# Gated linear attention with a gated projection on one core: attention in 64x64 blocks with a state at mid-chunk, one layout of v, y moved with its halo, and a new order of the work

## The chip, the cores and the metric

The kernel runs on one core of one Trainium2 chip. The metric is device time in microseconds (us), the median of several runs. Engines are named as in the profile: PE is TensorE (PEld its weight loads), DVE is VectorE, ACT is ScalarE, POOL is GpSimd, SP is SyncE, which only issues transfers here. In this kernel every engine's instructions are chained in the order in which the program is written, so each engine runs a fixed list.

## The reference

```python
f = 1 / (1 + exp(-f_logit))                       # B=4, H=8, S=768, D=48
for t in range(S):
    state = f[:, :, t, :, None] * state + einsum('bhd,bhe->bhde', k[:, :, t], v[:, :, t])
    y[:, :, t] = einsum('bhd,bhde->bhe', q[:, :, t], state)
x = y.transpose(0, 2, 1, 3).reshape(B, S, H * D)  # 4 x 768 x 384
gate = sigmoid(sum_k conv_w[k] * x shifted by 4 - k)   # 5 taps, per channel
out = (gate * (x @ w_val)) @ w_out                # two 384 x 384 products
```

## The kernel before

The 768 positions are six chunks of 128 (`NC`, `C`); a chunk is handled in two halves `h` of two batches each, and the eight heads of a batch lie as four pairs, one head on partitions 0 to 47 and one on 64 to 111. So a half holds eight pairs (`HP`).

Per chunk c the gates go through `pexp`, `pln`, a running sum (`csum` on PE in chunks 0 and 1, `scan` on DVE later) and `exp1`, `exp2`, the running product and its inverse; `pmulq` and `pmulk` scale q and k by them. With q and k scaled, a chunk's attention is plain products. `ktrans` transposes k on PE, `kevac` copies it out. `scores` makes k'q for 64-row blocks: the block on the diagonal, masked by `mask` (DVE), and the block of the first half of the chunk's keys against its second half of queries, copied by `cross` (ACT). `dstate` makes the whole chunk's addition to the state, which `stend` (DVE) adds and `stmul` (POOL) multiplies by the decay. `apply` sums four kinds of matmul into y: n = 0 and 1 from the state at the chunk's start, n = 2 and 3 from the masked blocks and v. Its output is written in 32-partition strips, in the place that x has in the projection, so that `xevac` (ACT) copies it straight to x (`XF`) and `halo` (POOL) copies the four positions before the chunk. For these strips v is loaded in two layouts, `vb` (in_v, with zero columns) and `vs` (in_vn).

The projection (numbered 0 to 4, and 5 and 6 for the two halves of the last chunk) takes x: `msplit` and `mlow` cut it in a high and a low part, `conv` (PE) or `mlast` and `mconv` (ACT, DVE) make the five taps, `gate` the sigmoid, `mval` the product with w_val, `mmul` the gating, `mhigh` and `mrest` the split of that, `mout` the product with w_out, `mstore` and `out` the result. The weights come as float64 and are rounded on the chip (`wload`, `weight`, eight steps each on POOL, ACT and DVE).

A float32 matmul is two records on PE with a weight load each; one in the split format (`mval`, `mout`) or a transpose is one. The whole order is one list, `PROGRAM`, of pieces such as `scores 1 2`: what is written first stands first on each engine that it uses. Loads are issued on SP with two rules (`begin`): each waits for the load four before it, and from the 16th on also for the PE instruction written just before it. `busy n` writes n matmuls on a constant, which nothing reads.

```python
for at, other in ((EARLY, PE.last), (FLIGHT, loads[n - FLIGHT] if n >= FLIGHT else None)):
```

All instructions carry the line of the helper that records them (L123 before, L140 after the change); tiles' names tell them apart: `banks<-qb,kb` is `scores`, `banks<-asb,vb` and `banks<-qb,st` are `apply`, `banks<-vs,ksb` is `dstate`, `banks<-ident,kb` is `ktrans`, `banks<-below,e` is `csum`, `banks<-xf,WD` is `conv`, `banks<-xH,wvT` is `mval`, `banks<-rg,woT` is `mout`, `banks<-keep` is `busy`.

Of the kernel before, what the change touches and what calls it, by code (L numbers as in the profile page):

```python
# [54 lines left out]
2; wload 4; loadw 0 1; loadq 1 0; wload 5; loadq 1 1; weight 0; pexp 0 2; pexp 0 1; pln 0 2; pln 0 1; csum 0 1; csum 0
2; exp2 0 0; pexp 1 0; exp1 0 0; exp2 0 1; pmulk 0 0; pmulq 0 0; pmulk 0 1; ktrans 0 0; exp1 0 1; pln 1 0; csum 1 0;
weight 1; exp2 0 2; exp1 0 2; pmulq 0 1; scores 0 1; kevac 0 0; pmulk 0 2; csum 1 1; dstate 0 0; exp2 1 0; weight 1;
exp1 1 0; okc 0; pmulq 0 2; scores 0 2; mask 0 1; weight 1; weight 1; weight 1; cross 0 1; weight 0; weight 0; weight
0; weight 0; weight 1; weight 0; scores 0 0; exp2 1 1; exp1 1 1; scores 0 3; mask 0 2; cross 0 2; ktrans 0 1; mask 0
0; cross 0 0; apply 0 0 3; pmulk 1 0; mask 0 3; pmulk 1 1; kevac 0 1; dstate 0 1; weight 2; weight 0; loadw 1 0; loadw  # L60
1 1; ktrans 1 0; weight 1; cross 0 3; weight 2; weight 1; weight 3; apply 0 0 2; ktrans 1 1; okc 1; weight 2; stend 0
1; stend 0 0; kevac 1 0; loadf 2 0; wload 6; apply 0 1 3; apply 0 1 2; pmulq 1 0; pmulq 1 1; xevac 0 0; weight 3;
weight 2; weight 2; weight 2; weight 3; weight 3; kevac 1 1; apply 1 0 0; scores 1 1; xevac 0 1; msplit 0; scores 1 0;
mask 1 1; weight 3; mask 1 0; dstate 1 1; dstate 1 0; weight 2; cross 1 1; scores 1 2; cross 1 0; apply 1 0 1; stend 1
1; stend 1 0; mlow 0; weight 3; pexp 2 0; pln 2 0; wload 7; loadv 1 1; loadk 2 0; loadk 2 1; loadw 2 0; apply 1 0 2;
apply 1 0 3; loadq 2 0; weight 2; weight 4; conv 0; weight 4; weight 3; xevac 1 0; scan 2 0; weight 4; mask 1 2; apply
1 1 0; cross 1 2; stmul 1 1; weight 3; weight 5; stmul 1 0; halo 1; exp2 2 0; exp1 2 0; loadf 3 0; loadq 2 1; loadv 3
0; loadw 2 1; wload 8; loadq 3 0; scores 1 3; loadv 2 0; loadk 3 1; loadv 2 1; loadk 3 0; gate 0 1; mval 0 1; mval 0
0; scan 2 1; weight 4; weight 4; pmulk 2 0; weight 5; gate 0 0; ktrans 2 0; exp2 2 1; weight 4; weight 5; weight 5;
mask 1 3; cross 1 3; mmul 0 0; exp1 2 1; weight 4; apply 1 1 1; apply 1 1 2; apply 1 1 3; mval 0 2; pmulk 2 1; weight  # L70
5; weight 5; pmulq 2 1; pmulq 2 0; ktrans 2 1; kevac 2 0; pexp 3 0; scores 2 0; xevac 1 1; mmul 0 2; apply 2 0 0; mmul
0 1; dstate 2 0; pln 3 0; kevac 2 1; scores 2 2; mask 2 0; cross 2 0; halo 2; weight 4; weight 6; scores 2 1; scan 3
0; mask 2 2; mask 2 1; dstate 2 1; msplit 1; cross 2 2; apply 2 1 0; weight 6; cross 2 1; scores 2 3; stend 2 0;
weight 6; weight 6; mask 2 3; weight 5; mhigh 0 0; exp2 3 0; cross 2 3; apply 2 1 1; apply 2 0 1; apply 2 0 2; apply 2
1 2; conv 1; apply 2 1 3; apply 2 0 3; weight 6; stend 2 1; weight 6; mrest 0 0; mlow 1; mhigh 0 1; exp1 3 0; mrest 0
1; mval 1 1; pmulk 3 0; mhigh 0 2; mrest 0 2; gate 1 0; stmul 2 0; weight 5; wturn 0; stmul 2 1; pmulq 3 0; apply 3 0
0; xevac 2 1; scores 3 0; xevac 2 0; scores 3 1; scan 3 1; okc 2; mlast 2 0; mmul 1 1; mconv 2 0 0; mlast 2 1; weight
6; weight 6; mconv 2 1 0; mconv 2 0 1; loadv 3 1; loadf 4 0; loadq 3 1; loadv 4 0; loadw 3 0; loadk 4 0; loadv 4 1;
loadw 3 1; mval 1 0; gate 1 1; mval 1 2; exp2 3 1; mask 3 0; cross 3 0; exp1 3 1; mmul 1 0; pmulk 3 1; mconv 2 1 1;
mask 3 1; mlast 2 2; cross 3 1; msplit 2; mout 0 0; ktrans 3 0; ktrans 3 1; mstore 0 0; mout 0 2; mmul 1 2; mconv 2 0  # L80
2; okc 3; mconv 2 1 2; pmulq 3 1; mconv 2 1 3; mconv 2 2 0; mconv 2 2 1; mconv 2 2 2; mconv 2 2 3; mout 0 1; pexp 4 0;
pln 4 0; kevac 3 0; mstore 0 2; mhigh 1 1; kevac 3 1; apply 3 0 1; apply 3 0 2; apply 3 0 3; mrest 1 1; scan 4 0;
apply 3 1 0; scores 3 3; xevac 3 0; scores 3 2; out 0 0; wturn 1; out 0 2; loadq 4 0; dstate 3 1; mask 3 2; mask 3 3;
mstore 0 1; mhigh 1 2; cross 3 2; dstate 3 0; cross 3 3; wturn 2; loadk 4 1; loadq 4 1; apply 3 1 1; apply 3 1 2;
apply 3 1 3; loadw 4 0; out 0 1; exp2 4 0; mhigh 1 0; exp1 4 0; stend 3 1; mrest 1 2; mrest 1 0; mconv 2 0 3; stend 3
0; pmulk 4 0; pmulq 4 0; stmul 3 1; stmul 3 0; halo 3; mout 1 0; mout 1 2; loadf 5 0; apply 4 0 0; gate 2; xevac 3 1;
halo 4; mlast 3 0; mlast 3 1; scores 4 0; scores 4 1; mstore 1 0; mlast 3 2; mstore 1 2; mlow 2; mval 2 0; loadq 5 0;
loadk 5 0; out 1 0; loadk 5 1; loadv 5 1; out 1 2; loadq 5 1; loadv 5 0; loadw 4 1; mval 2 2; mconv 3 1 0; mconv 3 0
0; scan 4 1; mconv 3 1 1; mmul 2 0; mconv 3 0 1; exp2 4 1; exp1 4 1; okc 4; mask 4 1; mout 1 1; cross 4 1; mmul 2 2;
mconv 3 2 0; pmulq 4 1; mask 4 0; pexp 5 0; pmulk 4 1; mhigh 2 0; ktrans 4 0; mval 2 1; mhigh 2 2; cross 4 0; pln 5 0;  # L90
kevac 4 0; apply 4 0 1; apply 4 0 2; apply 4 0 3; apply 4 1 0; ktrans 4 1; mmul 2 1; mhigh 2 1; mrest 2 0; mrest 2 2;
mrest 2 1; mout 2 1; scan 5 0; scan 5 1; mconv 3 0 2; mconv 3 2 1; mstore 1 1; mout 2 2; kevac 4 1; xevac 4 0; mstore
2 1; msplit 3; mlow 3; mout 2 0; scores 4 2; scores 4 3; mask 4 2; mask 4 3; mconv 3 0 3; out 1 1; out 2 1; exp2 5 1;
mstore 2 2; out 2 2; dstate 4 1; exp2 5 0; exp1 5 0; mstore 2 0; out 2 0; dstate 4 0; cross 4 2; cross 4 3; exp1 5 1;
apply 4 1 1; apply 4 1 2; apply 4 1 3; stend 4 1; stmul 4 1; pmulq 5 1; mconv 3 1 2; apply 5 1 0; mval 3 0; mconv 3 1
3; mconv 3 2 2; stend 4 0; mval 3 1; mconv 3 2 3; pmulk 5 1; pmulq 5 0; scores 5 2; xevac 4 1; gate 3; mlast 4 1; mmul
3 1; scores 5 3; pmulk 5 0; mval 3 2; halo 5; stmul 4 0; mlast 4 0; mask 5 3; cross 5 3; scores 5 0; mmul 3 0; mask 5
2; cross 5 2; mhigh 3 0; apply 5 1 1; apply 5 1 2; apply 5 0 0; apply 5 1 3; mmul 3 2; mrest 3 0; mhigh 3 2; mhigh 3
1; mlast 4 2; mrest 3 2; mrest 3 1; mout 3 1; mconv 4 0 0; mask 5 0; xevac 5 1; scores 5 1; cross 5 0; conv 6; mask 5
# [739 lines left out]
```

## Time and profile before

| what | us |
|---|---|
| median of 3 runs (lowest, highest) | 211.53 (209.95, 212.02) |
| the profiled execution, its span | 211.4 |
| its last matmul for the output ends | 204.1 |
| PE busy (records) | 182.7 (3732 and as many weight loads) |
| DVE busy | 145.5 |
| ACT busy | 130.2 |
| POOL busy | 36.6 |
| chain that ended last: PE, transfers, issue | 69%, 21%, 5% of the span |

The profiled execution is one run of the program and stands within 0.1 us of the median, so its rows add up to the time that is predicted. "Issue" in the chain is time in which an engine waited for nothing that the profile shows. The last 7.2 us of the span, from the last output's copy on, hold the landing of the last transfers and the test of a flag that sends rare inputs to a slow path.

### The profile page before, as it was taken

To read this page: it belongs to the slowest core of one execution; us is meant where nothing else is said; L and a number is where in the kernel's file an instruction comes from. 1 tells how busy PE (TensorE), PEld (TensorE's weight loads), DVE (VectorE), ACT (ScalarE), POOL (GpSimd) and SP (SyncE) were. 2 spreads that over 40 slices of the span, in tenths; PEclk is the share of its full clock that TensorE was granted. 3 is DMA by queue.
4 is the path that set the end of the run, shared out by engine and by line. 5 is a ranking of instruction groups with operands and counts; after the bars stand their busy time and mean duration, and the time that the engine had idled before them with its cause. 6 is when DMAs were issued, how large, how long until landed. Compare 5 with 4: busy or idle time off the path is not lost.

```text
span 211.4 us, 8218 instructions
## 1 busy us (share of the span) xinstructions
PE 182.7 (86%) x3732; PEld 149.6 (71%) x3732; DVE 145.5 (69%) x196; ACT 130.2 (62%) x188; POOL 36.6 (17%) x45
## 2 busy tenths in 40 slices
...
GB/s 197 334 264 342 346 368 210 284 8 289 319 363 381 288 15 3 6 99 409 338 286 122 288 240 173 386 352 108 6 2 3 6 3 101 0 3 3 132 215 11
DMA packets 12713, 38.61 MB, mean 183 GB/s; under 512 B 1537, under 2 KB 2945, under 8 KB 12161
## 3 DMA queue, kind: packets, MB, share of 16 engines
...
q8 instruction: 30, 0.49, 0.9%
...
## 4 chain that ended last, share of the span: by engine, by line
PE 69%; DMA 21%; issue 5%; SPq 1%; ACT 0%
PE banks L123 69%; DMA vb<-in_v 7%; DMA vs<-in_vn 6%; DMA qb<-in_q 3%; DMA raww<-in_wv 3%; DMA kb<-in_k 2%; SPq L123 1%; ACT qb L123 0%
## 5 line engine op out<-in xcount | busy, mean ns | idle before, releaser
L123 ACT ACTIVATE e<-e 112x1024 f32<-112x1024 f32 (+4 forms) x32 | 39.8, 1247 | 4.0 <-DMA e<-in_ft 3.4
L123 PE MATMUL banks<-xH,wvT 128*128 128x512 f32 x90 | 30.8, 404 | 0.0
L123 DVE SCALAR_TENSOR_TENSOR pre<-xf,cws,pre 128x512 f32<-128x512 f32 x36 | 27.3, 782 | 0.4
L123 PE MATMUL banks<-asb,vb 64*32 64x64 f32 (+3 forms) x1152 | 24.8, 261 | 2.1 <-issue 2.1
L123 PEld LDWEIGHTS banks<-asb,vb 64*32 64x32 f32 (+1 forms) x1152 | 22.4, 115 | 5.1 <-issue 4.1
L123 PE MATMUL banks<-rg,woT 128*128 128x512 f32 (+1 forms) x108 | 24.8, 371 | 0.0
L123 DVE TENSOR_TENSOR kb<-kb,e 112x1024 f32<-112x1024 f32 (+1 forms) x13 | 16.0, 1235 | 10.3 <-DMA kb<-in_k 10.3
L123 PE MATMUL banks<-vs,ksb 128*48 128x64 f32 x320 | 12.8, 242 | 11.6 <-DMA vs<-in_vn 5.9
L123 DVE TENSOR_TENSOR asb<-banks,tri 128x512 f32<-128x512 f32 x24 | 16.1, 683 | 7.7 <-PE banks L123 7.7
L123 PE MATMUL banks<-qb,kb 48*64 48x128 f32 (+1 forms) x768 | 19.8, 248 | 1.8 <-issue 1.8
L123 PEld LDWEIGHTS banks<-qb,kb 48*64 48x64 f32 x768 | 17.6, 133 | 5.1 <-issue 3.8
L123 POOL TENSOR_TENSOR st<-st,e 112x512 f32<-112x512 f32 x8 | 11.0, 1380 | 57.9 <-DVE st L123 34.6
L123 PEld LDWEIGHTS banks<-vs,ksb 128*48 128x48 f32 x320 | 11.4, 140 | 12.8 <-issue 10.1
L123 PEld LDWEIGHTS banks<-rg,woT 128*128 128x128 f32 x108 | 17.8, 188 | 3.4
L123 PEld LDWEIGHTS banks<-xH,wvT 128*128 128x128 f32 x90 | 16.9, 188 | 4.4 <-issue 0.2
L123 DVE TENSOR_TENSOR qb<-qb,e 112x1024 f32<-112x1024 f32 (+1 forms) x13 | 16.4, 1272 | 3.9 <-DMA qb<-in_q 2.3
L123 ACT COPY asb<-banks 128x256 f32<-128x256 f32 x24 | 8.8, 372 | 16.5 <-DVE asb L123 15.2
L123 DVE TENSOR_TENSOR_SCAN e<-keep,e 112x1024 f32<-112x1024 bf16 x8 | 18.3, 2304 | 0.0
L123 PE MATMUL banks<-xL,wvT 128*128 128x512 f32 x45 | 17.7, 394 | 0.0
L123 ACT COPY xf<-banks 128x768 f32<-128x768 f32 x12 | 9.6, 800 | 12.1 <-PE banks L123 11.9
L123 PE MATMUL banks<-xf,WD 32*32 32x512 f32 (+1 forms) x480 | 16.3, 486 | 0.4 <-issue 0.4
L123 DVE TENSOR_TENSOR gt<-banks,gt 128x512 f32<-128x512 f32 x15 | 10.1, 686 | 8.7 <-PE banks L123 7.0
...
## 6 DMA issues: line engine op xcount, KB each, us to landing
kb<-in_k SPq DMA_DIRECT2D x11, 512.0 KB, 6.3
qb<-in_q SPq DMA_DIRECT2D x11, 512.0 KB, 6.0
vb<-in_v SPq DMA_DIRECT2D x11, 512.0 KB, 5.7
vs<-in_vn SPq DMA_DIRECT2D x10, 512.0 KB, 6.1
...
```

The source lines that it names most:

```text
L123: ins = emit(*a, **kw)
```

## The change

`scores` makes only the two 64x64 blocks on the diagonal; what the first half of a chunk gives the second goes through a state at mid-chunk: `dstate` makes the addition of each 64 positions by itself, `smid` (DVE) adds the first to give `SM`, `stend` the second to give the next state. `cross` is gone, `mask` runs once per half on 1024 columns. `apply` sums masked blocks and v (n = 0, 1), and the states (n = 2 for the state that shares a row tile with the blocks, n = 3 for the other); between n = 3 and the other kinds PE waits for its own last matmul. All these run on 64x64 tiles of the array, also `ktrans` in two row tiles. y comes out by heads, not in x's places: `yevac` copies it to `YP` (one buffer per half), and six transfers `ymove` per half take it with its four halo positions to `XF`; `yhalo` carries the halo. v has one layout (`vs`, double buffered). PSUM's eight banks are one free list. A piece may name another engine (`yevac@1` is on DVE). The loads' layouts in memory are by batch. `PROGRAM` is a new list, with many single `busy`.

```diff
-        for i in range(HP):
-            PE.transpose(t[:, i * C : i * C + 112], kb[c % NB][:112, h * HP + i], ident[:112, :112])
...
+                PE.transpose(t[:, s, i * D : i * D + D], kb[c % NB][r, h * HP + i], ident[r, r], tile_position=(s * HC, 0))
...
+        ks, n = KSB[slot(c, h)], 2 if c < NC - 1 else 1
+        t = pair("d", c, h) if n == 2 else take("d", c, h).unsqueeze(1)
+        for i in range(HP):
+            for u in range(n):
+                for s in range(2):
+                    k = slice(u * HC, u * HC + HC)
+                    PE.matmul(t[rows(s), u, i * D : i * D + D], ks[k, s, i], vs[c % NB][k, h * HP + i, s * D : s * D + D],
+                              start=True, stop=True, tile_position=(u * HC, s * HC))
...
+    def smid(c, h):
+        if c:
+            DVE.tensor_tensor(out=SM[:, HS[h]], in0=ST[c % 2][:, HS[h]], in1=added(c, h, 0), op=ALU.add)
+        else:
+            DVE.tensor_copy(SM[:, HS[h]], added(c, h, 0))
...
+        DVE.tensor_tensor(out=ST[(c + 1) % 2][:, HS[h]], in0=SM[:, HS[h]], in1=added(c, h, 1), op=ALU.add)
...
-                        PE.matmul(t[at : at + HC, p & 1, o : o + C - u * HC],
-                                  kt[rows(s), b * NP + p, u * HC : u * HC + HC], qt[rows(s), b * NP + p, u * HC :],
-                                  start=True, stop=True, tile_position=(s * 64, at))
...
+                    PE.matmul(t[k, s, i * HC : i * HC + HC], kt[rows(s), h * HP + i, k], qt[rows(s), h * HP + i, k],
+                              start=True, stop=True, tile_position=(s * HC, u * HC))
...
-    def cross(c, b):
-
-        ACT.copy(ASB[aslot(c, b)][:, 2 * NP :].rearrange("p (u a) t -> p u a t", u=2),
-                 held["s", c, b][:].rearrange("p u (a t) -> p u a t", t=C)[:, :, 0:2, HC:])
-        done("s", c, b)
...
+                    if n < 2:
+                        lhs, rhs, row = vs[c % NB][k, bp, s * D : s * D + D], ASB[aslot(c, h)][k, s, b * NP + p], u
+                    elif c == 0 and u == 0:
+                        continue
                     else:
...
+                        lhs, rhs, row = (SM if u else ST[c % 2])[r, bp], qb[c % NB][r, bp, k], s
...
+            if j == 0 and prior is not None:
+                tc.add_manual_dep(ins.ins, prior.ins.name,
+                                  mybir.DependencyInfo(mybir.DependencyClass.Sync, mybir.DependencyReason.DATA),
+                                  reason="one bank, two row tiles")
...
-    def xevac(c, h):
-        t, b = held["x", c, h][:].rearrange("p a t -> p (a t)"), slice(2 * h, 2 * h + 2)
-        ACT.copy(XF[c % 2][:, :, b, HALO:], t[:, : 2 * NM * C].rearrange("p (g b t) -> p g b t", g=NM, b=2))
...
+    def yevac(c, h):
+        copy(ACT, YP[h][:, :, HALO:].rearrange("r i (u t) -> r u i t", u=2),
+             two("x", c, h)[:112].rearrange("r u (i t) -> r u i t", t=HC))
+        give("x", c, h)
+
+    def yhalo(c, h):
+        POOL.tensor_copy(YP[h][:, :, 0:HALO], YP[h][:, :, C : C + HALO])
+
+    MOVES = [(0, 48, 0), (64, 48, 48), (0, 32, 96, 0), (32, 16, 96, 1), (64, 16, 112, 1), (80, 32, 96, 2)]
+
+    def ymove(c, h, n):
+        r, k, to, *g = MOVES[n]
+        x = XF[c % 2][to : to + k, :, 2 * h : 2 * h + 2].rearrange("p m b t -> p m (b t)")
+        y = YP[h][r : r + k].rearrange("p (m b) t -> p m (b t)", b=2)
+        SP.dma_start(x[:, g[0]] if g else x, y[:, NM] if g else y[:, :NM])
...
+ktrans 1 1; kevac@1 1 1; weight 1; ymove 0 0 4; stmul 1 0; loadk 2 0; busy 1; busy 1; mask 1 0; apply 1 0 1;
```

PE, the first chunk, before (kb_66 and qb_64 hold k and q of even chunks, asb_83 and 84 masked blocks); the rows are written matmuls, two records each but for the transposes (`ident`):

```order
L123 MATMUL banks<-qb_64,kb_66 64x128 x4
L123 MATMUL banks<-qb_64,kb_66 64x64 x4
L123 MATMUL banks<-ident,kb_66 128x112 x8
L123 MATMUL banks<-asb_83,vb_68 32x128 x8
L123 MATMUL banks<-asb_83,vb_68 32x64 x8
L123 MATMUL banks<-asb_84,vb_68 32x128 x8
L123 MATMUL banks<-asb_84,vb_68 32x64 x8
L123 MATMUL banks<-vs,ksb_88 48x64 x16
```

PE, the same place after the change:

```order
L140 MATMUL banks<-qb_64,kb_66 64x64 x32
L140 LDWEIGHTS keep
L140 MATMUL banks<-keep 128x512
L140 MATMUL banks<-ident,kb_66 128x48 x16
L140 MATMUL banks<-qb_64,kb_66 64x64 x32
L140 LDWEIGHTS keep
L140 MATMUL banks<-keep 128x512
L140 MATMUL banks<-vs_68,ksb_87 48x48 x32
```

Columns of 64 or 48 take the place of 128 and 64, matmuls per piece double in `dstate` and `ktrans`, and single `busy` stand between the pieces.

DVE, chunk 3's attention, before (asb are masks, st the state, e the running sum of the gates, pre the convolution, rg the low part of the gated value):

```order
L123 SCALAR_TENSOR_TENSOR e_80<-keep,e_80 112x1024
L123 TENSOR_TENSOR asb_85<-banks,tri 128x512
L123 TENSOR_TENSOR asb_86<-banks,tri 128x512
L123 TENSOR_TENSOR st_74<-st_75,banks 112x512
L123 TENSOR_TENSOR rg_1052<-gt,rg_1051 128x512 x2
L123 SCALAR_TENSOR_TENSOR pre<-xf_89,cws,pre 128x512
L123 TENSOR_TENSOR st_74<-st_75,banks 112x512
```

DVE after the change, where chunk 4's attention is written:

```order
L140 TENSOR_TENSOR asb_85<-banks,tri 128x1024
L140 SCALAR_TENSOR_TENSOR e_81<-keep,e_81 112x1024
L140 TENSOR_TENSOR rg_1104<-gt,rg_1103 128x512
L140 TENSOR_TENSOR sm<-st_73,banks 112x384
L140 TENSOR_TENSOR st_74<-sm,banks 112x384
L140 SCALAR_TENSOR_TENSOR e_81<-keep,e_81 112x1024
L140 TENSOR_TENSOR asb_83<-banks,tri 128x1024
```

Two masks of 512 columns are one of 1024, and each step of the state is two (`sm`, `st`) of 384 in place of one of 512.

SP, the middle of the program, before:

```order
L123 DMA woN<-woT 32x2x384
L123 DMA kb_66<-in_k 128x1024
L123 DMA qb_64<-in_q 128x1024
L123 DMA vs<-in_vn 128x1024
L123 DMA out<-osb_96 128x512
L123 DMA e_81<-in_f 128x2048
L123 DMA qb_65<-in_q 128x1024
```

SP after the change, near the same place (yp_88 and 89 are the two halves' y, xf_91 is x of odd chunks):

```order
L140 DMA xf_91<-yp_88 32x264
L140 DMA out<-osb_97 128x512
L140 DMA xf_91<-yp_88 48x3x264
L140 DMA xf_91<-yp_89 32x264
L140 DMA xf_91<-yp_89 48x3x264
L140 DMA kb_67<-in_k 128x2x512
L140 DMA xf_91<-yp_89 32x264
```

The moves of y share one queue with loads and stores, each behind those written before it.

## Rows read from the trace of the kernel before

**Rows 1.** The page's DMA queues: packets, MB, share of 16 engines.

```profile
q8 instruction: 30, 0.49, 0.9%
```

**Rows 2.** The chain that ended last, in order of time: start, us, what.

```profile
23.87 6.57 DMA vs<-in_vn
...
30.58 10.57 PE banks L123 x278
41.15 2.60 issue
...
109.65 3.10 issue
```

**Rows 3.** Windows between issue stalls' ends: PE, PEld, DVE, ACT, POOL (count), clock, DMA, GB/s.

```profile
43.75:51.70 7.95, 7.53 (x255) 5.31 (x256) 7.06 (x8) 3.90 (x7) 4.35 (x3) 1.00 0.50 141
51.70:64.74 13.04, 11.66 (x256) 8.40 (x255) 11.42 (x14) 12.12 (x15) 6.29 (x4) 1.00 0.96 350
64.74:75.97 11.23, 9.46 (x253) 7.90 (x254) 8.46 (x10) 8.10 (x11) 3.92 (x5) 1.00 0.77 273
```

**Rows 4.** Windows by stage, the same columns.

```profile
0.00:30.58 30.58, 19.66 (x313) 16.26 (x313) 14.17 (x26) 20.68 (x33) 6.02 (x21) 0.92 0.90 307
30.58:173.83 143.25, 132.57 (x3127) 106.80 (x3128) 116.95 (x139) 95.52 (x125) 30.61 (x25) 0.95 0.54 187
120.00:160.00 40.00, 39.80 (x735) 32.43 (x737) 37.19 (x42) 27.67 (x37) 6.79 (x5) 1.00 0.50 177
173.83:204.20 30.37, 30.37 (x299) 26.54 (x293) 14.22 (x31) 13.60 (x30) 0.00 (x0) 1.00 0.18 67
```

**Rows 5.** Timeline, PE's weight loads from 16.9 to 27: start, us, tiles, count.

```profile
16.93 0.76 PEld L123 LDWEIGHTS banks<-qb,kb 48*64 48x64 f32 x32
...
17.76 1.80 PEld L123 LDWEIGHTS banks<-below,e 128*112 128x112 f32 x16
...
21.50 0.95 PEld L123 LDWEIGHTS banks<-vs,ksb 128*48 128x48 f32 x32 [1.95 <-DMA vs<-in_vn]
...
22.54 2.10 PEld L123 LDWEIGHTS banks<-qb,kb 48*64 48x64 f32 x96
...
24.88 0.78 PEld L123 LDWEIGHTS banks<-ident,kb 112*128 112x128 f32 x8 [0.24 <-ACT asb L123]
...
25.80 0.89 PEld L123 LDWEIGHTS banks<-asb,vb 64*32 64x32 f32 x64
```

**Rows 6.** Timeline, other stretches of one kind on PE and PEld.

```profile
2.26 3.26 PE L123 MATMUL banks<-keep 128*128 128x512 bf16 x8 [2.26 <-DVE keep L123]
...
38.35 0.40 PEld L123 LDWEIGHTS banks<-qb,st 48*32 48x32 f32 x32
...
46.05 0.38 PEld L123 LDWEIGHTS banks<-qb,st 112*32 112x32 f32 x16
...
46.40 1.77 PEld L123 LDWEIGHTS banks<-asb,vb 128*32 128x32 f32 x96
...
99.50 4.46 PE L123 MATMUL banks<-rg,woT 128*128 128x512 f32 x18
...
166.59 2.80 PE L123 MATMUL banks<-xf,WD 32*32 32x256 f32 x120
```

**Rows 7.** Groups on DVE, by shape: busy, mean ns, idle before.

```profile
L123 DVE TENSOR_TENSOR asb<-banks,tri 128x512 f32<-128x512 f32 x24 | 16.1, 683 | 7.7 <-PE banks L123 7.7
...
L123 DVE TENSOR_TENSOR kb<-kb,e 112x1024 f32<-112x1024 f32 x11 | 14.7, 1334 | 1.7 <-DMA kb<-in_k 1.7
...
L123 DVE TENSOR_TENSOR e<-banks,e 128x256 f32<-128x256 f32 x6 | 2.4, 419 | 6.1 <-ACT e L123 4.0 <-PE banks L123 2.1
```

**Rows 8.** Timeline, ACT's second exponential of the first chunk's gates.

```profile
5.36 0.95 ACT L123 ACTIVATE e<-e 128x896 f32<-128x896 f32 x1 [0.54 <-DMA e<-in_ft]
```

**Rows 9.** Groups on ACT, by shape: the exponentials from PSUM.

```profile
L123 ACT ACTIVATE e<-banks 112x1024 f32<-112x1024 f32 x6 | 6.0, 1034 | 0.0
```

**Rows 10.** Transfers: count, KB each, median us from issue to landing.

```profile
vb<-in_v SPq DMA_DIRECT2D x11, 512.0 KB, 5.7
...
woN<-woT SPq DMA_DIRECT2D x2, 192.0 KB, 6.5
```

More of the change, by code (lines that the diff above doesn't have):

```diff
@@ L55 @@
[L55 to L99, printed above, removed]
@@ new lines @@
+busy 1; busy 1; kevac 0 0; busy 1; loadv 0 0; pexp 1 0; pln 1 0; loadq 1 0; stmul 0 1; apply 0 1 2; wload 3;
+weight 1; loadk 1 0; dstate 0 0; smid 0 0; loadv 1 0; csum 1 0; exp2 1 0; busy 1; stend 0 0; pmulk 1 0;
+weight 0; apply 0 0 0; exp1 1 0; loadk 1 1; csum 1 1; apply 0 0 2; stmul 0 0; loadf 2 0; apply 0 1 3;
+yevac 0 1; ktrans 1 0; kevac@1 1 0; pmulq 1 0; dstate 1 0; apply 0 0 3; busy 1; smid 1 0; stend 1 0;
+ymove 0 1 0; exp2 1 1; pmulk 1 1; busy 1; ymove 0 1 2; ymove 0 1 1; wload 4; exp1 1 1; okc 1; weight 1;
@@ new lines @@
+weight 3; scores 1 1; ymove 0 1 3; loadq 2 0; loadk 2 1; ymove 0 0 3; mask 1 1; weight 3; ktrans 2 0;
+apply 1 0 2; kevac 2 0; dstate 2 0; ymove 0 0 2; wload 6; exp1 2 1; yhalo 1 1; stmul@1 1 1; loadf 3 0;
+apply 1 1 1; apply 1 1 2; apply 1 1 0; weight 2; weight 3; weight 3; weight 2; weight 2; exp1 2 0; weight 3;
+pmulq 2 0; yhalo 1 0; weight 2; weight 0; yevac@1 1 1; busy 1; scores 2 0; weight 3; mask 2 0; loadq 2 1;
+yevac 1 0; weight 3; msplit 0; weight 2; weight 4; weight 4; busy 1; loadv 2 1; ymove 1 1 2; ymove 1 1 5;
@@ new lines @@
+busy 1; busy 1; ymove 1 0 2; ymove 1 0 3; ymove 1 0 0; ymove 1 0 5; pmulk 2 1; mlow 0; smid 2 0; stend 2 0;
+pexp 3 0; pln 3 0; loadk 3 1; weight 4; weight 4; weight 4; conv 0; busy 1; ktrans 2 1; kevac 2 1; weight 3;
+weight 4; gate 0 2; apply 2 0 3; okc 2; gate 0 0; loadk 3 0; ymove 1 0 4; pmulq 2 1; scan 3 1; mval 0 2;
+scan 3 0; exp2 3 1; weight 4; exp1 3 1; mmul 0 2; busy 1; mhigh 0 2; dstate 2 1; pmulk 3 1; wload 7; wload 8;
+mval 0 1; mmul 0 1; scores 2 1; weight 5; weight 5; busy 1; mask 2 1; ymove 1 1 3; exp2 3 0; apply 2 0 1;
@@ new lines @@
+yhalo 2 0; yevac 2 0; busy 1; ymove 2 0 3; apply 2 1 3; yevac 2 1; busy 1; loadv 3 1; kevac 3 0; loadv 3 0;
+weight 6; weight 6; busy 1; conv 1; dstate 3 1; smid 3 1; weight 5; stend 3 1; ymove 2 1 1; ymove 2 1 0;
+ymove 2 0 1; loadq 4 1; scores 3 1; mask 3 1; pexp 4 0; pln 4 0; scan 4 1; scan 4 0; busy 1; ymove 2 1 2;
+ymove 2 0 0; gate 1 2; mval 1 2; apply 3 1 3; loadk 4 0; gate 1 0; dstate 3 0; smid 3 0; stend 3 0; mmul 1 2;
+loadq 4 0; ymove 2 0 2; mval 1 0; mmul 1 0; mval 1 1; mmul 1 1; apply 3 0 3; ymove 2 0 4; ymove 2 1 5;
@@ new lines @@
+ymove 2 0 5; exp2 4 0; exp1 4 0; ymove 2 1 4; pmulk 4 0; stmul 3 1; exp2 4 1; exp1 4 1; ymove 2 1 3; mlast 2 0;
+stmul 3 0; loadf 5 0; scores 3 0; mask 3 0; apply 3 1 0; mout 0 0; pmulq 4 1; ktrans 4 0; mstore 0 0;
+loadk 4 1; mlast 2 1; pmulq 4 0; mconv 2 1 0; loadv 4 0; mout 0 1; mconv 2 1 1; apply 3 0 2; apply 3 0 0;
+mconv 2 1 2; apply 3 1 1; kevac 4 0; msplit 2; mlow 2; pmulk 4 1; scores 4 0; mask 4 0; out 0 0; loadv 4 1;
+pexp 5 0; pln 5 0; yhalo 3 0; scan 5 1; mstore 0 1; apply 3 0 1; yevac 3 0; mout 0 2; mhigh 1 2; ktrans 4 1;
@@ new lines @@
+mrest 1 2; kevac 4 1; apply 3 1 2; dstate 4 0; mval 2 0; wturn 2; smid 4 0; stend 4 0; out 0 1; yhalo 3 1;
+mstore 0 2; mhigh 1 0; apply 4 0 3; ymove 3 0 4; ymove 3 0 3; mhigh 1 1; yevac 3 1; ymove 3 0 1; scan 5 0;
+exp2 5 0; ymove 3 0 5; exp2 5 1; out 0 2; ymove 3 0 0; ymove 3 1 5; ymove 3 1 0; loadk 5 1; scores 4 1;
+mask 4 1; ymove 3 1 2; dstate 4 1; mrest 1 0; mconv 2 1 3; ymove 3 0 2; mval 2 1; mval 2 2; ymove 3 1 4;
+ymove 3 1 1; smid 4 1; ymove 3 1 3; mrest 1 1; loadv 5 1; mlast 2 2; loadk 5 0; mconv 2 2 0; mconv 2 2 1;
```

364 lines of the change are left out of this document (195 added, 169 removed).

## The prediction

> **What bounds the kernel now.** I read the chain of waits in order of time first, then the busy time by windows, then the timeline of single stretches. Until 30.58 us the chain is made of loads; the last of them brings the second half of the first chunk's v, issued at 23.87 and landed at 30.44 [rows 2]. From there PE leads, with pieces of "issue" between: 2.60 at 41.15, 3.10 at 109.65 [rows 2]. I therefore cut the run in three: a start, a middle from 30.58 to the last `apply` matmul at 173.83 (143.25 long, PE busy 132.57, DVE 116.95), and a tail of 30.37 in which PE never stops [rows 4]; behind it come the 7.2 that the table gives for the end. The middle is where the change works.
>
> The issue pieces come from PE's own instruction stream. Between the ends of such stalls PE ran 255+256, 256+255 and 253+254 records [rows 3], each time two lots of 256, and the instruction queue brought 0.49 MB in 30 packets [rows 1], about 16 KB each. So a stall comes when a block of 256 is used up before the next is there. The quickest two blocks took 7.95, 4.0 each, and those under a DMA share of 0.96 took 6.5 each [rows 3].
>
> **PE's work.** Prices per record, from stretches of one kind: scores 2.10/96 = 21.9 ns at 96 columns on the mean; `dstate` 0.95/32 = 29.7; transposes 0.78/8 = 97; 64-row, 32-column products 0.89/64 = 13.9 [rows 5]; `apply` per half 0.40 and 0.38 for the states, 1.77 for the blocks [rows 6]. Before: scores 768 x 21.9 = 16.8; blocks 12 x 1.77 = 21.2; states 10 x 0.78 = 7.8; `dstate` 10 x 0.95 = 9.5; transposes 10 x 0.78 = 7.8; in all 63.1.
>
> After, by the order: 768 records of scores, 768 of blocks, 704 of states, 704 of `dstate`, all with 64 or 48 columns on four tiles, and 192 transposes of 48 columns. By columns a score falls to 21.9 x 64/96 = 14.6, and the nearest row, the 13.9 above, says nearly the same. I take 14.6 for the scores (11.2) and 13.9 for the others (30.2); a transpose 97 x 48/112 = 42, halved because two row tiles work side by side, 21 (4.0). In all 45.4, **17.7 less**. The bounds: with 21.9 for every record and 42 a transpose it is 72.5, a loss of 9.4; with the quickest row, 0.40/32 = 12.5 [rows 6], also for transposes, 39.2, a gain of 23.9.
>
> The Trainium skill, "TensorEngine Tiling (Array Packing)", section "Performance Considerations", speaks against the change: each matmul carries some 60 cycles, and a tiling factor should not come out of a dimension that is already small. At 2.4 GHz that would be 25 ns a record, 74 for these 2,944 records by an estimate from that page. The 12.5 and 13.9 of the rows lie under it, so between records on different tiles the trace doesn't bear it out.
>
> **Other terms of the middle on PE.** (1) PE's work between 16.93, the first scores, and 30.58 belongs to the new middle, because that begins with the first scores: six stretches, 0.76 + 1.80 + 0.95 + 2.10 + 0.78 + 0.89 = +7.3 [rows 5]; 16 more running-sum records stand behind the first scores now, +1.8 at the 1.80 of that row. (2) Behind the last `apply` now stand two more `mout` (18 matmuls, 4.46) and one more half `conv` (120 records, 2.80) [rows 6]: -7.3 here, +7.3 in the tail. (3) 31 `busy` stand in the middle. Eight took 3.26, 0.41 each; a 512-column matmul takes 4.46/18 = 0.25 [rows 6]. At 0.25 they are +7.7; if all of them fall in waits, 0. (4) PE waits for itself between kinds of `apply`, 13 times by the order. No row has such a wait; that it gains time is excluded, since it only holds PE back, and I put it between 0 and 0.4, the length of the short stretches [rows 6]; at 0.3: +3.9. (5) 4,113 records with their loads are 762 instructions more than 2 x 3,732, three blocks; at 1.5 a block, half of the longer stalls, +4.4. If the stalls vanish it is -10. Sum: 143.3 - 17.7 + 7.3 + 1.8 - 7.3 + 7.7 + 3.9 + 4.4 = **143.4** on PE.
>
> **DVE.** `mask`: 24 of 0.683 become 12 of 1024 columns; 256 columns cost 0.419 and 512 cost 0.683 [rows 7], so 1024 cost 1.21: -1.9. `smid` is new, 12 of 384 columns at 0.55: +6.6; `stend` falls from 0.68 to 0.55, ten times: -1.3; one `stmul` comes from POOL: +0.6. Copies that the order puts on DVE instead of ACT, by the same slope: three `yevac` 3.6, two `kevac` 1.9, four of 512 columns 2.7, four of 256 columns 1.7: +9.9. In all **+13.9**. Moved: of the 14.2 of the start all but some 1.3 fall into the new middle (+12.9); behind the last `apply` stand 25, by the order and the prices above, where there were 14.2 [rows 4], -10.8. DVE in the middle: 117.0 + 12.9 - 10.8 + 13.9 = **133.0**.
>
> So 133.0 of DVE must fit beside 143.4 of PE. At its densest DVE was busy 37.19 of 40, 0.93, and over the whole middle 116.95 of 143.25, 0.82 [rows 4], there waiting for PE. At 0.93 the middle is 143, at 0.82 it is 162. I take 0.90, nearer the dense stretch, because PE, which made it wait, is lighter: **147.8**. ACT loses `cross` and part of its copies and has slack.
>
> **Start, transfers, tail.** The first scores wait for the gates' chain: the exponential of the second part starts at 5.36 and takes 0.95 [rows 8], the logarithm as much, 16 running sums 1.80 [rows 5], an exponential 1.03 [rows 9], two products of 1.33 [rows 7]: 5.36 + 0.95 + 0.95 + 1.8 + 1.03 + 2.67 = 12.8, with a little between them **13.0**, against 16.93. v's second layout was 11 loads of 512 KB and two halves [rows 10], 6.3 MB; at the start's 307 GB/s [rows 4] those of the first chunk alone are 3.4 us, so v comes in time for `dstate` and the wait that ended at 30.44 goes. What is late next is the instruction stream. The 72 moves of y are costed at nothing in the middle: transfers between buffers on chip land in 6.5 [rows 10], and the projection runs most of a chunk behind its attention. Without that cover it is 6.5 a half; behind each move on SP stand loads, and behind `yevac` the halves' one buffer. Tail: 30.4 + 7.3 + three `busy` (0.6) = **38.3**; end 7.2.
>
> 13.0 + 147.8 + 38.3 + 7.2 = 206.3; I predict **206**, 2.5% below the 211.4 of the profiled run and its median of 211.5.
>
> **The rivals.** *A. The instruction stream no longer stalls*, because the new list spreads dense records among long matmuls. Then PE's middle falls under DVE's 143, and DVE at 0.95 needs 140: 198.5. For it: in the last 30 us no block stalls. Against: the first two chunks hold some 2,180 instructions with hardly a long matmul. The Trainium skill, "Runtime: NRT & Kernel Launch", section "Instruction fetch mechanics", is on this side: blocks of 256 instructions, and crossing one mostly hidden. By that the stalls should not be there now; the 2.60 and 3.10 say otherwise. *B. Gains and additions cancel*: DVE at 0.87 makes 152.9 and 211.4. *C. DVE is fed no better than before and, with more work, holds the end*: at 0.82 the middle is 162 and the time 220.5. Its place is DVE's fixed list between mask, `smid`, `stend` and the convolution steps: one late PE product delays all behind it. It decides from a busy share under 0.87. *D. The stream is the bound*: the middle's 3,612 records are 28.2 blocks; at 5.6, as between 64.74 and 75.97 [rows 3], 158 and 216.5. It decides from 5.4 a block. *E. Short records cost as long ones*, the bound of 21.9: PE's middle 171, 229.
>
> **How the numbers follow.** Forecast (200 to 209.3) 0.38; A 0.17; B 0.15; C 0.18; D 0.09; E 0.03. A difference under 1% can hardly be told from none here: below 209.4 is faster, 0.55; to 213.6 the same, 0.15; above, slower, 0.30. The range must take in A with 2 us below it and most of C: 195 to 219.
>
> **What would show it.** First scores near 13 and v no longer on the chain; scores near 14 ns a record in a clean stretch; DVE busy near 159 in all (145.5 + 13.9) with 0.90 of the middle; stalls marked issue, once per 256 records, mostly before 80 us; the last `apply` near 161. The forecast is wrong if DVE's share of the middle is nearer 0.82, if chains of DVE, PE and POOL through the two states leave both idle, or if `ymove` ends waits of `msplit` or `conv`.

## The result, and the profile after

The change makes the kernel **3.1% faster**: 204.53 us (203.9 to 205.1, 4 runs) against 211.78 in the runs beside it, ratio 0.969 with a 95% interval of 0.962 to 0.976. The profiled execution took 203.9 with a span of 202.2. Forecast: 206, range 195 to 219. Ratios leave out runs that were some per cent slower than the fastest of the same kernel; the medians with their ranges, and the profiles of experiments 2, 4, 8 and 9, take in such runs.

From the page of the kernel after, busy time by engine with its share of the span, and the shares of the chain that ended last:

```profile
PE 183.0 (90%) x4113; PEld 142.6 (71%) x4113; DVE 155.1 (77%) x210; ACT 115.8 (57%) x151; POOL 38.0 (19%) x52
...
PE 70%; DMA 6%; DVE 6%; issue 4%; ACT 3%; SPq 3%; POOL 1%; POOLq 0%; ACTq 0%
```

PE is busy as long as before, 183.0 against the 182.7 of the table. The span is 9.2 shorter, so all of it came out of PE's idle time: 28.7 before, 19.2 now.

The windows by stage (the columns of rows 3 and 4): first up to the first scores, then the middle up to the last `apply` and the tail up to the last matmul for the output; below, the middle again in three parts.

```profile
0.00:13.95 13.95, 10.42 (x67) 6.13 (x67) 3.67 (x7) 9.54 (x17) 2.85 (x18) 1.00 0.81 249
13.95:157.60 143.65, 134.46 (x3614) 104.71 (x3614) 126.23 (x155) 92.29 (x107) 35.11 (x34) 0.93 0.67 207
157.60:195.30 37.70, 37.70 (x434) 31.71 (x432) 25.01 (x50) 13.97 (x29) 0.00 (x0) 1.00 0.26 87
...
13.95:40.00 26.05, 22.79 (x664) 16.97 (x664) 13.83 (x24) 11.70 (x13) 2.17 (x3) 0.87 0.64 203
40.00:60.00 20.00, 15.44 (x541) 13.52 (x541) 19.46 (x25) 9.19 (x13) 5.85 (x7) 0.66 0.75 233
60.00:157.00 97.00, 95.63 (x2400) 73.73 (x2402) 92.44 (x107) 70.80 (x82) 27.09 (x25) 1.00 0.67 202
```

These six lines make three regimes. Until 40 neither PE nor DVE is full. From 40 to 60 DVE is (19.46 of 20), and PE waits part of the time and runs at a granted clock of 0.66 on the mean. From 60 on both nearly are: PE 0.986, DVE 0.953. Which of the two holds the end there can't be read from such shares; the experiments had to tell.

From the chain of waits in order of time (start, us, what), the places where PE waited for its own instructions, and two where a transfer led:

```profile
16.42 2.09 PE banks L140 x80
18.51 1.54 issue
20.05 13.11 PE banks L140 x297
...
39.98 0.91 issue
...
52.63 5.59 DMA xf<-yp
...
65.06 0.48 issue
...
86.56 4.96 DMA vs<-in_vn
91.52 0.14 issue
91.66 104.03 PE banks L140 x2039
```

The load of v that ended at 30.44 before [rows 2] is gone from the start. The stalls are shorter than the 2.60 and 3.10 of before [rows 2], and from 91.66 on PE leads without a break.

### The profile page after: what moved, and what is told of

The parts are those of the page before. It is cut to its first block, busy times and chain, and to the rows that moved or that the text cites. A ratio compares the mean times of both kernels' runs of the same rounds, so it can differ in the third digit from the quotient of the medians.

```text
span 202.2 us, 9138 instructions
## 1 busy us (share of the span) xinstructions
PE 183.0 (90%) x4113; PEld 142.6 (71%) x4113; DVE 155.1 (77%) x210; ACT 115.8 (57%) x151; POOL 38.0 (19%) x52
## 4 chain that ended last, share of the span: by engine, by line
PE 70%; DMA 6%; DVE 6%; issue 4%; ACT 3%; SPq 3%; POOL 1%; POOLq 0%; ACTq 0%
PE banks L140 70%; DMA xf<-yp 4%; SPq L140 3%; DMA vs<-in_vn 2%; ACT e L140 1%; DVE work L140 1%; DVE qb L140 1%; DVE e L140 1%; DVE kb L140 1%; ACT yp L140 1%; POOL yp L140 1%; DVE asb L140 1%; POOL WD L140 0%; DVE gt L140 0%; ACT rg L140 0%
## 5 line engine op out<-in xcount | busy, mean ns | idle before, releaser
L140 ACT ACTIVATE e<-e 112x1024 f32<-112x1024 f32 (+4 forms) x32 | 39.1, 1241 | 17.8 <-DVE e L140 11.9
L140 DVE TENSOR_TENSOR kb<-kb,e 112x1024 f32<-112x1024 f32 (+1 forms) x13 | 15.3, 1187 | 10.9 <-ACT e L140 10.9
L140 PE MATMUL banks<-keep 128*128 128x512 bf16 x53 | 18.9, 451 | 2.3 <-DVE keep L140 2.3
L140 PEld LDWEIGHTS banks<-xH,wvT 128*128 128x128 f32 x90 | 16.9, 188 | 4.1
L140 PE MATMUL banks<-qb,sm 48*48 48x64 f32 x384 | 17.3, 232 | 1.6 <-issue 0.9
L140 PE MATMUL banks<-asb,vs 64*48 64x64 f32 x768 | 16.7, 237 | 1.6 <-DVE asb L140 1.6
L140 PEld LDWEIGHTS banks<-asb,vs 64*48 64x48 f32 x768 | 14.4, 135 | 4.9 <-issue 2.5
L140 PEld LDWEIGHTS banks<-qb,sm 48*48 48x48 f32 x384 | 14.2, 128 | 5.1 <-issue 2.9
L140 POOL TENSOR_TENSOR st<-st,e 112x384 f32<-112x384 f32 x9 | 10.0, 1107 | 39.4 <-DVE st L140 21.8
L140 PE MATMUL banks<-vs,ksb 64*48 64x48 f32 x704 | 13.3, 226 | 3.3 <-issue 1.5
L140 DVE TENSOR_TENSOR asb<-banks,tri 128x1024 f32<-128x1024 f32 x12 | 14.6, 1218 | 1.4 <-PE banks L140 1.1
L140 PEld LDWEIGHTS banks<-vs,ksb 64*48 64x48 f32 x704 | 12.0, 139 | 5.1 <-issue 3.6
L140 PE MATMUL banks<-qb,kb 48*64 48x64 f32 x768 | 15.0, 228 | 0.3 <-issue 0.3
```

What stands on the lines that cost most here:

```text
L140: ins = emit(*a, **kw)
```

## The experiments

Each was timed against the kernel before, run on the same chip beside it; "against after" compares its ratio with 0.969. Differences to after of 1% or less lie within the intervals.

Single profiles differ more than that early in the run. The first stall, 1.54 at 18.51 in after, is between 1.09 and 3.46 in experiments 1, 2, 4 and 6, whose edits act only behind it; here it is in experiment 1:

```profile
18.37 3.46 issue
```

The first `conv` starts at 60.8 in after and at 63.8 in experiment 1, whose edit acts behind 107 us. So some comparisons below run from the first `conv` to the end.

**1. Half of the convolution steps left out, in after and in before.** The same edit in both lists, for chunks 2 to 4:

```diff
-mconv 2 1 0; mconv 2 1 1; mconv 2 1 2; ... mconv 2 1 3
+mconv 2 1 0; mconv 2 1 2
```

> After, with half of the convolution steps on VectorE (steps 1 and 3 of each channel tile in chunks 2 to 4) left out: 18 operations of 0.76 us, 13.7 of VectorE, some two thirds of it before 160 us; the gate of these chunks is computed from fewer taps. T1, VectorE is the bound between 40 and 160 us (busy 114.8 of 120): the time falls by 6 to 10 us. T2, TensorE with its instruction stream is the bound there (busy 114.1 of 120): 0 to -2. T3, each waits for the other in turn: -3 to -5.

> The kernel before, with the same 18 convolution steps of 0.78 us left out. If VectorE was not its bound (busy 101 of 120 between 40 and 160 us, 0.84), 0 to -3 us; if VectorE held its end through the order of its work, -6 or more.

Measured: after without them 205.19 (203.06 to 206.82), ratio 0.966 (0.955 to 0.976), which is after's time. Before without them 0.995 (0.989 to 1.002), also the same. The first kernel's busy time by engine from its page, then the window from the first `conv` to the end in it and in after, in the columns of above:

```profile
PE 179.0 (88%) x4113; PEld 140.0 (69%) x4113; DVE 144.1 (71%) x192; ACT 116.3 (57%) x151; POOL 35.0 (17%) x52
```

```profile
63.80:203.80 140.00, 133.24 (x2842) 106.08 (x2841) 104.24 (x140) 84.87 (x110) 22.85 (x22) 0.99 0.52 161
60.80:202.20 141.40, 133.69 (x2841) 105.88 (x2841) 117.30 (x158) 84.57 (x110) 26.29 (x24) 0.99 0.53 163
```

DVE lost 11 us of work in all and 13 in this stretch, PE's busy time stayed, and 1.4 us was gained. T1 falls and T2 has its 0 to -2: behind 107 us, where all of these steps stand, DVE is nearly full and yet not what sets the time.

**2. Scores of chunks 2 to 5 issued twice, in after and in before.** In after (before alike, around its own matmul):

```diff
+                    for _ in range(2 if c > 1 else 1):
-                    PE.matmul(t[k, s, i * HC : i * HC + HC], kt[rows(s), h * HP + i, k], qt[rows(s), h * HP + i, k],
+                        PE.matmul(t[k, s, i * HC : i * HC + HC], kt[rows(s), h * HP + i, k], qt[rows(s), h * HP + i, k],
```

> After, with every scores matmul of chunks 2 to 5 issued twice into the same place: 512 more records with their loads, 7 to 8 us of TensorE at 14.6 ns and four more instruction blocks; nothing else changes. T1, VectorE is the bound: +0 to +4. T2, TensorE or its instruction stream is the bound: +7 to +12. T3: +4 to +7.

> The kernel before, with every scores matmul of chunks 2 to 5 issued twice: 512 more records of 21.9 ns, 11.2 us, and four more instruction blocks. If TensorE led from 30.58 us on, as the chain says, +10 to +17; if it only shared the bound, +3 to +8.

Measured: after 222.85 (220.26 to 224.79), ratio 1.047 (1.036 to 1.058), some 16.5 us above after; before 227.42, ratio 1.075 (1.066 to 1.084), some 16 above before. Both are over PE's own time for the records. One doubled half of the first, PE's weight loads (start, us, tiles, count), and its chain behind 80 us:

```profile
77.79 2.10 PEld L140 LDWEIGHTS banks<-qb,kb 48*64 48x64 f32 x128 [0.36 <-ACT e L140]
```

```profile
81.38 0.78 issue
82.16 4.22 PE banks L140 x126
86.39 0.60 issue
86.99 12.11 PE banks L140 x370
99.09 1.40 issue
100.49 21.22 PE banks L140 x607
121.72 1.60 issue
123.31 9.03 PE banks L140 x239
132.35 0.62 issue
132.96 27.89 PE banks L140 x743
160.85 2.00 issue
```

128 records took 2.10, so 512 cost 8.4; the six stalls add up to 7.0, where after has 0.14 behind 80 us. Together 15.3 of the 16.5. The window from the first `conv` to the end:

```profile
65.50:222.00 156.50, 143.07 (x3290) 115.68 (x3289) 115.21 (x158) 82.72 (x107) 17.44 (x21) 0.98 0.46 144
```

It is 15.1 longer than the 141.40 of after, 9.4 of it in PE's busy time and 5.7 in its idle time. So PE is the bound, as T2 said, though the price is above its +7 to +12 and has two parts: a record's own 16 ns, and instruction blocks that come late once the stretches get denser, somewhat less than that again. Four blocks were added, so it is 4.1 for each with its records. In the kernel before, the sign that PE led, +10 to +17, came. The Trainium skill, "Runtime: NRT & Kernel Launch", section "Instruction fetch mechanics", has the crossing of a block mostly hidden; after comes near that behind 66 us, this kernel doesn't.

**3. Short fills.** The 45 single `busy` keep their places in the list:

```diff
-            PE.matmul(banks[:, free[i % len(free)]], keep[:, 0], keep[:, 0:4], start=True, stop=True)
+            b, m = banks[:, free[i % len(free)]], keep[:, 0:4].rearrange("p a t -> p (a t)")
+            x = 512 if n > 1 else 32
+            PE.matmul(b[:, :x], keep[:, 0], m[:, :x], start=True, stop=True)
```

> After, with each of the 45 single fills (busy 1) cut from 512 columns to 32; they stay in the list, so the instruction blocks are the same. 32 of them stand before 60 us, where TensorE waits for others, 13 behind it. Theory P, now that the first four runs point to TensorE as the bound behind 60 us: the 13 give back 0.25 us each, 3 us, and those before 60 us nothing: -2 to -4. Theory Q, the long fills keep the granted clock up: it falls below the 0.65 to 1.00 of now in more stretches and the time grows by 1 to 6 us. Theory R, VectorE is the bound throughout: 0 within 1.

Measured: 203.10 (201.68 to 205.62), ratio 0.962 (0.954 to 0.969), the lowest median of all, though its interval overlaps after's, so that a gain isn't shown. Its PE is busy 178.5 in all, 4.5 less. A fill lasts 189 ns instead of 390 in the median. Its windows before 60 us:

```profile
13.95:40.00 26.05, 22.11 (x695) 19.89 (x691) 15.72 (x28) 13.62 (x18) 2.18 (x3) 0.78 0.65 221
40.00:60.00 20.00, 15.17 (x527) 13.12 (x523) 19.55 (x22) 9.46 (x11) 6.80 (x9) 0.60 0.74 222
```

The granted clock is lower, 0.78 and 0.60 where after had 0.87 and 0.66: the condition of Q came, its loss didn't. The profiled run is 2.2 shorter than after's, and 1.8 of that stands before the first `conv` (59.0 for 60.8), where P had put nothing; behind it the 13 fills gave back 0.4 (141.0 for 141.4) instead of 3. So P fails in its place as well.

**4. Three steps off VectorE before 61 us.**

```diff
-yevac@1 0 0; ... stmul@1 1 1; ... yevac@1 1 1
+yevac 0 0; ... stmul 1 1; ... yevac 1 1
```

> After, with three steps before 61 us taken off VectorE: two copies of y (1.22 us each) go to ScalarE, one product of the state (0.57) to GpSimd: 3.0 us less on VectorE in the stretch from 36 to 63 us, in which it never waits. Theory P, VectorE is the bound there and TensorE behind 60 us: -1.5 to -3. Theory R, VectorE throughout: also -1.5 to -3, so that only the first four runs tell the two apart. Theory S, neither but the order of the steps: 0, or a loss up to 2 because the copies arrive later on ScalarE.

Measured: 205.68 (202.98 to 206.15), ratio 0.969 (0.959 to 0.979): no gain, though the interval leaves room for one of 1.5. In the stretch itself DVE is now idle for some of the time, and PE does no more than before:

```profile
40.00:60.00 20.00, 15.27 (x520) 12.75 (x518) 17.36 (x22) 10.42 (x13) 5.70 (x6) 0.68 0.73 216
```

From the end of the first stall to the first `conv` are 41.0 us (21.2 to 62.2), in after 40.7 (20.05 to 60.76). So a full DVE was not by itself the bound from 40 to 60 either, as far as this profile shows. Nor was PE's low clock: the run of experiment 1 had 0.83 from 40 to 60 for after's 0.66, with the same list, and took 42.0 for the same way. S is left, chains between the engines. Which one ends last there stays open.

**5. Transfers and loads doubled into their own place.** Both were meant to price a resource and priced a wait instead.

```diff
+        for _ in range(2):
-        SP.dma_start(x[:, g[0]] if g else x, y[:, NM] if g else y[:, :NM])
+            SP.dma_start(x[:, g[0]] if g else x, y[:, NM] if g else y[:, :NM])
```

```diff
-        "loadv": lambda c, h: load(vs[c % NB][:, HS[h]], vn, c, h * HP, h * HP + HP),
+        "loadv": lambda c, h: [load(vs[c % NB][:, HS[h]], vn, c, h * HP, h * HP + HP) for _ in range(2)],
```

> After, with every transfer of y within the chip issued twice in a row: 72 more transfers with the same contents, 4.8 MB more within the chip, and 72 more issues on SyncE. If the moves are hidden, as the prediction had it: 0 to +2. If they stand on the path, at 3.2 to 3.7 us a landing and the loads queued behind them: +4 to +12.

> After, with every load of v issued twice: 12 more loads of 384 KB, 4.7 MB more of reads, in the place of the second layout that the change dropped. If the dropped loads are what started the middle earlier: +3 to +8, most of it before 60 us. If the transfers have room: 0 to +2.

Measured: 370.0, ratio 1.75, and 224.59, ratio 1.054 (1.042 to 1.066). What SyncE waited for in the first (total, times, longest), then in the second:

```profile
SPq L140 <- DMA xf<-yp: 160.3, 72, 6.2
```

```profile
SPq L140 <- DMA vs<-in_vn: 52.1, 13, 5.8
```

The second transfer writes what the first writes, so SyncE stands until the first has landed, 72 times 2.2 us in the one, and every load behind it stands with it. Neither says whether the doubled resource was free.

**6. The moves doubled aside.** The second copy goes to a tile of its own:

```diff
         SP.dma_start(x[:, g[0]] if g else x, y[:, NM] if g else y[:, :NM])
+        z = XD[to : to + k, :, 2 * h : 2 * h + 2].rearrange("p m b t -> p m (b t)")
+        SP.dma_start(z[:, g[0]] if g else z, y[:, NM] if g else y[:, :NM])
```

> After, with a second transfer behind each transfer of y that copies the same piece into a tile that nobody reads, so that it needn't wait for the first to land, as it had to where both wrote the same place: 72 more transfers, 4.8 MB. If the moves are hidden, as the prediction had it: 0 to +2, and what grows is SyncE's issuing alone. If their issuing and their share of the DMA engines is on the path: +4 to +10, from loads that come later and instruction blocks that come later.

Measured: 236.38 (234.77 to 238.97), ratio 1.112 (1.098 to 1.125), some 30 above after: far more than expected. Its page's chain, and its issues of the second copies (ns min/median/max):

```profile
PE 37%; SPq 23%; DMA 17%; issue 6%; DVE 5%; ACT 5%; POOL 1%; ACTq 0%; DVEq 0%; another core or an unknown queue 0%
```

```profile
L140 SPq DMA_DIRECT2D xd<-yp x72: 546/598/1803, 35.2 to 198.7; - x72
```

SyncE's own issuing is now 23% of the chain, in after it is 3%. A move keeps SyncE for 0.6 us in the median, so 72 of them are some 43 us of its queue, and the chain has loads that start behind rows of them. The loads themselves land as before (v 4.8 us, in after 5.0). But the copies also read `YP`, of which each half has one buffer, so `yhalo` waits longer for the moves (57.1 us for 33.3) and `yevac` for `yhalo` (16.7 for 2.8). How the 30 us divide between the issuing and these waits isn't shown.

**7. Before without v's second layout.** All `loadw` leave the list, and `vs` is set once:

```diff
+    POOL.memset(vs, 0.5)
...
-loadw 0 0; ... loadw 4 1
```

> The kernel before without the second layout of v: all 12 of its loads (6.3 MB) are left out, and the tile that they fill is set once to a constant, so the state is computed from that constant. Theory L, the loads held the start: the 16.9 of the first scores and the wait that ends at 30.44 shrink, -4 to -8, as much as the whole change gave (6.5); the attention in 64x64 blocks then gave nothing of its own. Theory M, the gain is TensorE's lighter attention: 0 to -3, because other loads or the instruction blocks are late next.

Measured: 207.47 (205.14 to 209.3, 4 runs) against 212.80 (209.68 to 217.64, 8 runs); no interval was worked out, but all four lie below all eight, the lowest runs differ by 4.5 and the medians by 5.3. By the trace it is ten loads of 512 KB that are left out, 5.2 MB, not twelve of 6.3; the change itself drops the other of the two layouts, `vb`. From its page, and PE's weight loads for one half of the last chunk's scores in it, against those of before and of after:

```profile
PE 181.3 (89%) x3732; PEld 149.1 (73%) x3732; DVE 145.8 (71%) x196; ACT 130.2 (64%) x188; POOL 40.3 (20%) x46
```

```profile
149.03 1.43 PEld L124 LDWEIGHTS banks<-qb,kb 48*64 48x64 f32 x64 [0.36 <-issue]
```

```profile
155.22 1.43 PEld L123 LDWEIGHTS banks<-qb,kb 48*64 48x64 f32 x64 [0.36 <-issue]
```

```profile
139.26 1.05 PEld L140 LDWEIGHTS banks<-qb,kb 48*64 48x64 f32 x63
```

PE's idle time falls from 28.7 to 23.3. Its first scores and the `dstate` that waited for v, then that `dstate` in the kernel before:

```profile
17.24 0.76 PEld L124 LDWEIGHTS banks<-qb,kb 48*64 48x64 f32 x32
...
28.41 1.39 PEld L124 LDWEIGHTS banks<-vs,ksb 128*48 128x48 f32 x32 [0.17 <-ACT wvT L124]
```

```profile
30.55 1.76 PEld L123 LDWEIGHTS banks<-vs,ksb 128*48 128x48 f32 x32 [3.86 <-issue]
```

Theory L holds in size: dropping the loads alone is worth some 5 of the whole change's 7. It holds less in place: the first scores come no earlier (17.24 for 16.93), the `dstate` comes 2.1 earlier, and the last chunk's scores 6.2, so that more of the gain arises behind the start than in it. After reaches its last chunk ten us sooner still, but its tail is longer, and in the end it is only some 1 to 3 ahead of this kernel.

**8. Fewer loads under way.**

```diff
-EARLY, FLIGHT = 16, 4
+EARLY, FLIGHT = 16, 3
```

> After, with at most 3 instead of 4 loads under way at a time. Theory F, TensorE's instruction blocks are late where many loads are under way: the stalls marked issue shrink (1.54 at 18.51 to under 1) and the time falls by 1 to 3 us. Theory G, the loads themselves are needed that early: the start and the waits for q, k and v grow, +2 to +8.

Measured: 205.12 (203.47 to 208.16), ratio 0.960 (0.953 to 0.968): not to be told from after. The first stall was 1.91 at 20.13, not shorter, but by the range given above one profile can't decide that. F isn't borne out, G neither.

**9. Short fills and two queues for the moves.** The edit of 3, and

```diff
-        SP.dma_start(x[:, g[0]] if g else x, y[:, NM] if g else y[:, :NM])
+        (ACT if n > 3 else SP).dma_start(x[:, g[0]] if g else x, y[:, NM] if g else y[:, :NM])
```

> After with the 45 single fills cut from 512 columns to 32, and the two smallest of the six transfers of y of each half (24 of 72) issued from ScalarE's queue instead of SyncE's: at a median 0.60 us of issuing each, 14 us off SyncE's queue. Theory U, SyncE's issuing holds back loads behind 60 us (doubling the transfers cost some 30 us): together with the fills -3 to -5 against after, about 200. Theory V, at single transfers SyncE has room and only the fills count: -1 to -2.5. Theory W, ScalarE, in whose order the transfers now wait for the halo, loses what SyncE gains: 0 or slower than after.

Measured: 204.70 (202.87 to 208.97, 6 runs), ratio 0.975 (0.967 to 0.983): no faster than after, and above experiment 3. U falls, and V's -1 to -2.5, a ratio of 0.964 to 0.957, lies below the interval too. W is left, 0 or slower: either SyncE's issuing held nothing back, or ScalarE lost what SyncE gained, and this run can't tell them apart. For the first speaks what SyncE waited for in after (total, times, longest):

```profile
SPq L140 <- PE banks L140: 41.3, 26, 9.8
```

It stands 41.3 us in waits for PE, and only 21.8 with the moves doubled. None of these kernels beats after beyond its interval.

## Why the prediction was right, and where its steps were not

**The sum.** Start 13.95 against 13.0, middle 143.65 against 147.8, tail 37.70 against 38.3, end 6.9 against 7.2. The span was 202.2, the sum 206.3: the middle makes up nearly all of the difference. The sum is one of a span, and the prediction took it for the time. In every run that lists both, the time is 1.7 to 2.1 us above the span, so 206.3 stands for a time near 208. That the forecast of 206 came within 1.5 of the 204.53 is in part luck.

**What sets the middle.** This is the step that failed. The prediction let DVE set it, 133.0 at a share of 0.90. DVE had 126.2 there, a share of 0.88, but experiment 1 shows that 13 us less of it give 1.4 and experiment 2 that more on PE costs in full. PE sets the time from 91.66 us on, where the chain has nothing else; from 72 to 91.5 the chain runs through moves, DVE and a load, and from 40 to 60 what sets it stays open. The DVE sum came near by two errors: at 0.88 its 133.0 would have made 151, but DVE had 6.8 less to do there, 2.4 of it left in the start and 4.3 not there at all (155.1 in all for 159.4).

PE's own sum, 143.4, stands 0.3 from the middle as it came out, and would have given 13.0 + 143.4 + 38.3 + 7.2 = 201.9. That too is luck. By its terms PE is busy 124.4 (132.6 - 17.7 + 7.3 + 1.8 - 7.3 + 7.7) and idle 19.0 (10.7 + 3.9 + 4.4); it was busy 134.5 and idle 9.2. Two misses of 10 us cancel.

**PE's prices.** A clean stretch of after, PE's weight loads:

```profile
109.32 0.99 PEld L140 LDWEIGHTS banks<-asb,vs 64*48 64x48 f32 x62
...
110.20 1.05 PEld L140 LDWEIGHTS banks<-qb,kb 48*64 48x64 f32 x63
111.12 0.57 PEld L140 LDWEIGHTS banks<-asb,vs 64*48 64x48 f32 x32
```

From start to start 62 records of the blocks take 0.88, 14.2 ns each, and 63 of the scores 0.92, 14.6: the prices forecast, 13.9 and 14.6. `dstate` took 11.9 (64 from 91.62 to 92.38), and only a transpose was mis-sized, 39 ns (16 from 114.07 to 114.69) for 21, 3.5 us in all. So rival E falls, and the 25 ns that the prediction worked out from the Trainium skill, "TensorEngine Tiling (Array Packing)", section "Performance Considerations", don't hold here between records on different tiles.

**What ate the 17.7.** PE is busy no less than before. The transposes are 3.5 of the 10 us of busy time too much; how the rest divides isn't shown. The fills are part of it: 53 of them last 18.9 added up (such times overlap others), where eight were 3.3. The prediction gave them 7.7 on the path; shortened, they gave back 2.2 in the profiled run, 1.6 by the ratio, which the intervals don't tell from nothing. The clock may be another part. Windows of two us behind the first stall (the eighth column is the granted clock):

```profile
18.00:20.00 2.00, 0.51 (x8) 0.18 (x8) 0.00 (x0) 1.78 (x2) 0.00 (x0) 0.88 0.98 334
20.00:22.00 2.00, 1.95 (x59) 1.50 (x59) 0.47 (x1) 1.71 (x2) 0.00 (x0) 0.50 0.99 339
...
26.00:28.00 2.00, 2.00 (x85) 1.92 (x85) 0.43 (x1) 0.00 (x0) 0.00 (x0) 0.91 0.04 8
```

and in it 64 records of the blocks:

```profile
22.75 1.74 PEld L140 LDWEIGHTS banks<-asb,vs 64*48 64x48 f32 x64 [0.84 <-issue]
```

PE stood nearly still from 18.3 to 20, the granted clock fell to 0.50, the level of 1.2 GHz, and came back after 26; a block record cost 27 ns in place of 14. By these prices, as an estimate, a stall of 1.54 cost up to 3 us more behind it (6.4 us at half speed). A longer stretch at 0.50, from about 43.5 to 57, follows a wait of PE for a mask; the wait, and a window of it:

```profile
44.35 0.89 PEld L140 LDWEIGHTS banks<-asb,vs 64*48 64x48 f32 x32 [2.12 <-DVE asb L140]
```

```profile
45.00:55.00 10.00, 8.21 (x293) 7.54 (x288) 9.89 (x11) 4.05 (x5) 1.88 (x2) 0.50 0.84 252
```

No term of the sum had the clock. But the middle before had such stretches too: its mean was 0.95 [rows 4], after's is 0.93, which is some 3 us over 143 by an estimate, and experiments 1 and 3 show a higher clock without gain and a lower one without loss before 60 us. So this part is small, if there is one.

**Loads.** That v comes in time was right (PE waits 0.6 us for it once), and 13.0 for the first scores nearly so. Experiment 7 shows that the loads alone, dropped from the kernel before, give most of the gain. The prediction had the wait for v in its start, but called the middle, with PE's lighter attention, the place where the change works. What the attention gives by itself wasn't tried, since its tiles and the order hang together; gains needn't add up, so that the loads carry 5 of the 7 in after too is not shown.

**Moves.** Costed at nothing: they landed in 3.2 to 3.7 rather than 6.5, and dividing them between two queues gave nothing. The sign that was to tell, waits of `msplit` or `conv` that they end, is 1.7 us in two waits. But they end others, of `yhalo` for the one buffer (total, times, longest):

```profile
POOL yp L140 <- DMA xf<-yp: 33.3, 8, 16.5
```

Two landings, 5.59 and 2.47, stand on the chain of after, and SyncE's issuing, of loads too, with 3% of the span. So the cover mostly holds, and it is thin. That the prediction missed: it named the loads behind them on SyncE and the one buffer, but priced landings, not the issuing, and twice as many moves cost 30 us.

**Stalls.** The shape was right (1.54 at 18.51, 0.91 at 39.98, 0.48 at 65.06, none behind 91.66), the size too high: +4.4 for three blocks on top of those before, where all four of after's add up to 3.1, less than the 5.7 of the two in rows 2. Rival A's stream came true behind 66 us, not its time of 198.5, which it took from DVE; its reason, dense records between long matmuls, fits experiment 2. Rival D has no place in after (143.65 for 28.2 blocks, 5.1 each), but experiment 2 moves the kernel towards it. Rival C's long DVE list was there; that it was the bound fell with experiment 1, behind 107 us.
